# Strided sparse attention and a rational MLP: new transfer times and landing allowance in the planner, casts released by the preceding batch's loads, constant matmuls in TensorE's early rests

## The chip, the core and the metric

The kernel runs on one core of a Trainium2 chip. The metric is the device time of one execution in microseconds (us). Below, PE is the matrix engine (TensorE), DVE the vector engine, ACT the scalar engine, POOL the engine that issues casting DMAs here, and SP the engine that issues the other DMAs. The first three compute; POOL and SP hardly do anything but issue transfers. Each engine runs its own instructions strictly in the order in which the program lists them, and waits at an instruction until the semaphores that it names have their counts.

## The reference

Attention over 8 batches of 8 heads with 576 positions of 64 values, followed by an MLP on all 4608 tokens (512 wide, 2048 in the middle) whose activation is a ratio of polynomials. The first four heads (kind L) see the last 32 positions; the other four (kind S) see every 32nd position.

```python
rel = pos[:, None] - pos[None, :]
mask_local = (rel >= 0) & (rel < stride)
mask_strided = (rel >= 0) & (pos[None, :] % stride == pos[:, None] % stride)
...
attn = np.exp(scores)
attn = attn / (np.sum(attn, axis=-1, keepdims=True) + 1e-09)
return np.matmul(attn, v).astype(np.float32)
...
h = x @ w_in
P = a[0] + a[1] * h + a[2] * h2 + a[3] * h3
Q = 1.0 + np.abs(b[0]) * np.abs(h) + np.abs(b[1]) * h2
g = P / (Q + 1e-06)
return (g @ w_out).astype(np.float32)
```

The heads' outputs of a token, side by side, are its row of x.

## The kernel before

**Who sets the order.** No engine's order is written out by hand. The functions below record operations (`P.op`) with an engine, a planned duration, a key and the tiles that they read and write. `schedule` then places them: it keeps a planned time for each engine, takes the operation that is ready with the smallest key, and assigns PSUM banks on the way. A DMA has two planned times: what its issue takes on the issuing engine, and `dma=`, what the transfer takes in that engine's queue; it counts as landed (`o.fin`) 2.2 us after its transfer ends. So a planned time costs nothing itself. It decides what stands before what on each engine.

**Stages of a batch b.** `casts(b)` issues from POOL the transfers that turn q, k and v from float32 to bfloat16. For batches 0 and 1 (`b < NPE`) they go to SBUF and PE transposes them (`loads_pe`, L615 and L652, copied out at L634, L636, L664, L666). From batch 2 on, `bulk` (L517) casts in DRAM: five transfers (q, k, v for the L heads, q, k for the S heads), and two more (L572) bring v of the S heads straight to the tile vS. `loads(b)` then issues from SP two DMA transposes of q and k for each kind (L681, tiles tq, tk), four copies that swap halves of tq and tk (L692) and five loads of v (L705, L709, tile vL). `attention(b)` works on four units, L, S, S, L. Each has scores on PE (L791, L800 for L; L876, L884 for S), their negated maximum on DVE (L810, L891), its addition on PE (L817, L898), the exponential on ACT (L823, L904), a transpose of the probabilities (tiles ptL, ptS; by PE for batches 0 and 1, L835 and L916 with copies at L721 and L723; by a DMA transpose from SP after that, L841 and L924), the product with v on PE (L853; L947 with sums L934), and the division on DVE (L862, L864; L954, L957). `turn` transposes the result on PE (L747, L754), and ACT copies it into XT (L770).

**MLP.** As soon as 512 tokens (a chunk c) are in XT, `mlp1(c)` and `mlp2(c)` are recorded. `mlp1` makes two groups of eight products (L982, 4 matmuls each, copied by ACT at L988 to a tile h), and on each group of 128x4096 values DVE does nine operations (L1008, L1010, L1012, L1039, L1041 to L1045) and ACT two (L1036 Ln, L1038 Exp). `mlp2` multiplies with the second weight (L1071), ACT copies to a tile os (L1083, four in turn) and POOL stores it (L1090). The last group of the last chunk is cut up, with parts of its activation on ACT (L1004 to L1031).

**Waits that the recording adds.** `after=` makes an operation wait for others besides those of its tiles. `casts(b, after)` takes seven such lists, one for each cast and each half of vS. `loads(b, pace=land)` makes the first transposes of batch b wait for `land[0]`, the landed transposed probabilities of the first unit of the batch before, the copies and v loads for `land[1]`, and the second transposes for `land[2]`. In the main loop the casts of batch 3 wait partly for the loads of batch 2 and partly for its `land`, and those of batches 4 to 7 for `land` of the batch two before.

**Constant matmuls.** `filler` (L136 of the profile) issues matmuls on a tile FL of constants into a PSUM bank that nobody uses. `schedule` puts them where PE's plan has a rest over 0.5 us ahead of an operation with a key below −1e9 (no operation has one) or at least 8*512+2250 (the last chunk's second product): `int(rest * 0.75 / 0.216)` of them, none at time 0.

Of the kernel before, what the change touches and what calls it, by code (L numbers as in the profile page):

```python
# [84 lines left out]
class Prog:  # L85
# [65 lines left out]
    def schedule(self):  # L151
# [7 lines left out]
        free = {e: 5.0 if e == "pool" else 0.0 for e in self.ENG}  # L159
# [61 lines left out]
        while left:  # L221
# [23 lines left out]
            if e == "pe" and (o.key < -1000000000.0 or o.key >= (8 * 512 + 2250)) and t - free[e] > 0.5:  # L245
                spare = [i for i in range(8) if not held[i] and bank_free[i] <= free[e] + 0.2]
                if spare:
                    i = spare[-1]
                    n = int((t - free[e]) * 0.75 / 0.216) if free[e] > 0 else 0
                    if n:  # L250
                        bank_free[i] = max(bank_free[i], t)
                        f = self.filler(n, i, bank_tile[i], t)
                        if bank_tile[i] is None:
                            bank_tile[i] = PTile("fl", 1)
                            bank_tile[i].ops.append(f)
            free[e] = t + o.dur
            if o.dma is not None:
                at = max(dmafree[e], t + o.dur)
                busy = any(v > at for k, v in dmafree.items() if k != e)
                dmafree[e] = at + o.dma * (2 if busy else 1)  # L260
                o.fin = dmafree[e] + 2.2
            else:
                o.fin = t + o.dur
# [106 lines left out]
def bass_strided_sparse_attn__then__act_rational_pade_kernel(nc, q, k, v, moe_w_in, moe_w_out, moe_a, moe_b, out):  # L370
# [143 lines left out]
    def bulk(s_t, d_t, b, h0, nh, hd, t, key, after):  # L514
# [5 lines left out]
            0.7, key, w=[t], dma=1.65 * nh / 4, after=after)  # L520
# [14 lines left out]
    def casts(b, after=None):  # L535
# [6 lines left out]
        for n in range(2):  # L542
            if b < NPE and n:
# [5 lines left out]
                    0.8, key, w=[vt], dma=0.8, after=vl.prev)  # L549
                for h in range(HL):  # L550
# [4 lines left out]
                        1.1, key, w=[vt], dma=1.6, after=vl.prev)  # L555
# [3 lines left out]
            for i, (s_t, d_t, t) in enumerate(((q, q16, T_q[b][n]), (k, k16, T_k[b][n]))):  # L559
                if b >= NPE:  # L560
# [6 lines left out]
                    0.8, key, w=[t], dma=2.0, after=list(after[3 * n + i]) + h.prev)  # L567
# [3 lines left out]
        for x in range(2):  # L571
# [4 lines left out]
                0.9, key, w=[vS], dma=2.0, after=after[5 + x])  # L576

    def weights_in():
        FH = Fmid // 2
        for i in range(2):  # L580
            T_win[i].new()
            for kk in range(NK1):
                P.op("pool", lambda e, kk=kk, i=i: e.dma_start(
                    Win[:, kk, FH * i:FH * i + FH], w_in[kk * 128:(kk + 1) * 128, FH * i:FH * i + FH]),
                     0.8, -9e4, w=[T_win[i]], dma=1.4)

    def weights_out(after=()):
        T_wout.new()
        for j in range(4):
# [3 lines left out]
                0.8, -4e4, w=[T_wout], dma=3.3, after=after)  # L593
# [505 lines left out]
    for b in range(B):  # L1099
# [4 lines left out]
        if b == NPE:  # L1104
            g = [cur["ops"]] * 3 + [[land[0]]] * 2 + [[land[1]]] * 2
            casts(b + 1, g)
        if NPE <= b + 1 < B:
            st = loads(b + 1, pace=land if b >= NPE else None)
        if b >= NPE and b + 2 < B:
            casts(b + 2, [[land[i]] for i in ((1, 2, 2, 3, 3, 3, 3) if b == NPE else (0, 0, 1, 2, 2, 3, 3))])  # L1110
# [49 lines left out]
```

## Time and profile before

| | us |
|---|---|
| three runs, median (lowest, highest) | 427.37 (423.12, 430.69) |
| the profiled execution, its time | 427.88 |
| its span | 426.1 |
| PE busy | 376.9 (88%) |
| DVE busy | 359.2 (84%) |
| ACT busy | 291.9 (69%) |
| POOL busy | 70.7 (17%) |
| DMA transfers, median from issue to landing: transpose of q or k / of ptL / of ptS | 6.6 / 3.6 / 3.8 |
| the same, cast of q / of k / of v in DRAM | 6.2 / 7.7 / 5.7 |

The profile is of one execution. "Busy" is the time in which an engine executes; the rest is waiting or idle. The span runs from the first instruction to the end of the last; the execution's time is 1.78 us longer. PE's busy time counts matmuls as their records show them, with ends that are modelled; a mean of 393 ns stands for one of the 128x512 matmuls, which follow each other every 0.22 us at full clock. "Granted clock" is the share of its full clock that PE was given. A line such as L982 is a line of the program; a group of one line is one kind of instruction.

### The profile page before, as it was taken

What the parts mean: (1) busy time and instruction counts of PE and PEld (TensorE: products, weight loads), DVE (VectorE), ACT (ScalarE), POOL (GpSimd) and SP (SyncE); (2) the same over time, 40 slices, a digit from 0 to 9 for tenths busy, and PEclk for the clock granted to TensorE, in tenths of its full rate; (3) what the DMA queues carried; (4) which work ended last, traced back from release to release, by engine and by line L of the source; (5) the groups of instructions that cost most, each with busy time, mean ns of one, the idle gap of its engine ahead of it and who ended that gap; (6) DMA issues with size and microseconds to landing.
All of it is one profiled execution on the core that took longest, in us unless ns stands there. A gap on an engine that the chain in (4) does not pass through costs nothing.

```text
span 426.1 us, 8697 instructions
## 1 busy us (share of the span) xinstructions
PE 376.9 (88%) x3842; PEld 190.8 (45%) x3842; DVE 359.2 (84%) x315; ACT 291.9 (69%) x316; POOL 70.7 (17%) x112
## 2 busy tenths in 40 slices
PE   2777959989978598999998899989989999999796
PEld 2353536435534354554544355545444443344242
DVE  3471699999996128989999988999999999999992
ACT  2253795679465057778676848798587987989971
POOL 8951001001330012121030102000200200101100
PEclk9996996999975799899999989999999999999999
DMA  9999999106999999999699935901310110200202
GB/s 105 186 187 192 223 153 144 29 2 114 189 184 136 131 205 145 156 233 148 128 224 152 114 57 141 196 2 51 100 31 2 57 43 25 75 2 0 100 0 98
DMA packets 101830, 47.48 MB, mean 111 GB/s; under 512 B 89280, under 2 KB 97728, under 8 KB 101312
## 3 DMA queue, kind: packets, MB, share of 16 engines
q0 software_dynamic: 20384, 27.05, 36.4%
q1 hardware_dynamic: 81408, 19.87, 30.2%
q8 instruction: 30, 0.49, 0.5%
q14 instruction: 8, 0.07, 0.0%
HBM read 40.18 MB, written 18.28 MB: 137 GB/s over the span
## 4 chain that ended last, share of the span: by engine, by line
DVE 45%; PE 27%; ACT 10%; DMA 10%; issue 5%; SPq 3%; DVEq 0%; POOLq 0%
PE PSUM L982 9%; PE PSUM L1071 8%; DVE u L1012 6%; DVE h L1045 5%; DVE z L1043 5%; DVE u L1010 4%; ACT u L1036 4%; DMA ptS<-pS 4%; DVE z L1008 3%; DVE z L1041 3%; DVE xS L957 3%; DVE z L1042 3%; DVE z L1039 3%; ACT u L1038 3%; DVE z L1044 3%
## 5 line engine op out<-in xcount | busy, mean ns | idle before, releaser
L982 PE MATMUL PSUM<-XT,Win 128*128 128x512 bf16 x576 | 141.3, 393 | 4.0 <-ACT h L988 2.6
L1071 PE MATMUL PSUM<-Wout,h 128*128 128x512 bf16 x576 | 136.5, 388 | 6.3 <-DVE h L1045 4.0
L988 ACT ACTIVATE h<-PSUM 128x512 bf16<-128x512 f32 x144 | 83.0, 602 | 42.9 <-PE PSUM L982 42.9
L1071 PEld LDWEIGHTS PSUM<-Wout,h 128*128 128x128 bf16 x576 | 55.5, 99 | 73.2 <-DVE h L1045 3.8
L982 PEld LDWEIGHTS PSUM<-XT,Win 128*128 128x128 bf16 x576 | 54.0, 101 | 73.8 <-ACT h L988 11.4
L1036 ACT ACTIVATE u<-u,consts 128x4096 bf16<-128x4096 bf16 x17 | 63.1, 3710 | 15.2 <-DVE u L1012 15.2
L1038 ACT ACTIVATE u<-u 128x4096 bf16<-128x4096 bf16 x17 | 61.5, 3619 | 0.4
L1090 POOL DMA_DIRECT2D out_dram<-os x32 | 21.9, 686 | 179.6 <-ACT os L1083 179.6
L1012 DVE TENSOR_TENSOR u<-u,z 128x4096 bf16<-128x4096 bf16 x18 | 41.2, 2292 | 0.5
L1043 DVE TENSOR_TENSOR z<-z,h 128x4096 bf16<-128x4096 bf16 x17 | 39.0, 2291 | 0.5
L1041 DVE TENSOR_TENSOR z<-z,h 128x4096 bf16<-128x4096 bf16 x17 | 38.9, 2290 | 0.5
L1045 DVE TENSOR_TENSOR h<-z,u 128x4096 bf16<-128x4096 bf16 x17 | 38.9, 2286 | 0.4
L1083 ACT ACTIVATE os<-PSUM 128x512 f32<-128x512 f32 x34 | 19.2, 600 | 18.4 <-PE PSUM L1071 18.4
L1008 DVE TENSOR_SCALAR z<-h 128x4096 uint16<-128x4096 uint16 x17 | 20.6, 1213 | 12.7 <-ACT h L988 12.7
L770 ACT ACTIVATE XT<-PSUM 128x576 bf16<-128x576 bf16 (+2 forms) x40 | 19.8, 556 | 11.4 <-PE PSUM L754 8.8
L517 POOL DMA_DIRECT2D q<-in_q_dram x12 | 7.3, 610 | 110.2 <-DMA ptL<-pL 70.9
L891 DVE TENSOR_REDUCE ng<-PSUM 100x16 bf16<-100x576 f32 x16 | 11.9, 751 | 15.8 <-PE PSUM L884 15.8
L1010 DVE TENSOR_SCALAR u<-z,coef 128x4096 bf16<-128x4096 bf16 x18 | 24.1, 1338 | 0.4
L823 ACT ACTIVATE pL<-PSUM 128x960 bf16<-128x960 f32 x16 | 15.5, 966 | 12.2 <-PE PSUM L817 12.2
L1039 DVE TENSOR_SCALAR z<-h,coef 128x4096 bf16<-128x4096 bf16 x17 | 22.9, 1345 | 0.5
L904 ACT ACTIVATE pS<-PSUM 100x576 bf16<-100x576 f32 x16 | 10.2, 646 | 18.2 <-PE PSUM L898 18.1
L1044 DVE TENSOR_SCALAR z<-z,coef 128x4096 bf16<-128x4096 bf16 x17 | 21.8, 1284 | 0.5
(80 smaller groups left out, 394.0 us busy)
## 6 DMA issues: line engine op xcount, KB each, us to landing
out_dram<-os POOLq DMA_DIRECT2D x32, 256.0 KB, 3.2
q<-in_q_dram POOLq DMA_DIRECT2D x12, 288.0 KB, 6.2
k<-in_k_dram POOLq DMA_DIRECT2D x12, 288.0 KB, 7.7
vS<-in_v_dram POOLq DMA_DIRECT2D x16, 144.0 KB, 9.2
vL<-v SPq DMA_DIRECT2D x24, 96.0 KB, 6.1
Win<-in_moe_w_in_dram POOLq DMA_DIRECT2D x8, 256.0 KB, 12.7
Wout<-in_moe_w_out_dram POOLq DMA_DIRECT2D x4, 512.0 KB, 23.6
v<-in_v_dram POOLq DMA_DIRECT2D x6, 288.0 KB, 5.7
```

What stands on the lines that cost most here:

```text
L982: r = e.matmul(ph.f, Win[:, kk, f * 128:(f + 1) * 128], XT[:, kk, xc:xc + CH], start=(kk == 0), stop=(kk == NK1 - 1))
L988: P.op("act", lambda e, f=f, ph=ph, h=h: e.activation(h.t[:, f % G, :], ph.f, AF.Copy), 0.6, key, r=[ph], w=[h])
L1010: dv(lambda e, zz=zz, uu=uu: e.tensor_scalar(uu, zz, b1_ap, b0_ap, op0=Alu.mult, op1=Alu.add), ts + 0.28, r=[z, T_b], w=[u])
L1012: dv(lambda e, zz=zz, uu=uu: e.tensor_tensor(uu, uu, zz, op=Alu.mult), tt, r=[z], m=[u])
L1036: P.op("act", lambda e, uu=uu: e.activation(uu, uu, AF.Ln, bias=eps1, scale=1.0), 0.833 * W / 1000 + 0.28, key, r=[T_co], m=[u])
L1038: P.op("act", lambda e, uu=uu: e.activation(uu, uu, AF.Exp, scale=-1.0), 0.833 * W / 1000 + 0.19, key, m=[u])
L1039: dv(lambda e, zz=zz, hh=hh: e.tensor_scalar(zz, hh, a_ap[3], a_ap[2], op0=Alu.mult, op1=Alu.add), ts + 0.28, r=[h, T_co], m=[z])
L1041: dv(lambda e, zz=zz, hh=hh: e.tensor_tensor(zz, zz, hh, op=Alu.mult), tt, r=[h], m=[z])
L1043: dv(lambda e, zz=zz, hh=hh: e.tensor_tensor(zz, zz, hh, op=Alu.mult), tt, r=[h], m=[z])
L1044: dv(lambda e, zz=zz: e.tensor_scalar(zz, zz, a_ap[0], None, op0=Alu.add), ts + 0.22, m=[z])
L1045: dv(lambda e, zz=zz, hh=hh, uu=uu: e.tensor_tensor(hh, zz, uu, op=Alu.mult), tt, r=[z, u], m=[h])
L1071: r = e.matmul(po.f, h.t[:, j, m * 128:(m + 1) * 128], Wout[:, kk, :], start=(kk == 0), stop=(kk == NF - 1))
```

## The change

Four edits. The planned issue and transfer times of the POOL transfers are other numbers, POOL starts at 3.5 instead of 5.0 in the plan, and a DMA that is issued in the plan after 12 us counts as landed 1.5 us later, after 60 us 9 us later. The casts of batch 3 wait for the loads of batch 2 alone (the last vL load and the transposes of k of both kinds), those of batch b + 2 for the loads of batch b + 1; the loads no longer wait for `land`. Constant matmuls are also put into planned rests before operations with a key below 1300 (batches 0 and 1, the first products of chunk 0, and the scores at the head of batch 2), 0.7 of the rest instead of 0.75, and 16 of them ahead of PE's first operation. In the program as built there are 36 of them in the head (16, 8, 2, 2, 5, 3), and at the end 31 and 7 where there were 27 and 15.

```diff
--- before.py
+++ after.py
@@ -156,7 +156,7 @@
                 d.users.append(o)
         pend = {e: [] for e in self.ENG}
         avail = {e: [] for e in self.ENG}
-        free = {e: 5.0 if e == "pool" else 0.0 for e in self.ENG}
+        free = {e: 3.5 if e == "pool" else 0.0 for e in self.ENG}
         order = self.order = {e: [] for e in self.ENG}
         dmafree = {e: 0.0 for e in self.ENG}
         for o in list(self.ops):
@@ -242,11 +242,11 @@
             if at > t:
                 heapq.heappush(pend[e], (at, o.key, o.idx, o))
                 continue
-            if e == "pe" and (o.key < -1000000000.0 or o.key >= (8 * 512 + 2250)) and t - free[e] > 0.5:
+            if e == "pe" and (o.key < 1300 or o.key >= (8 * 512 + 2250)) and t - free[e] > 0.5:
                 spare = [i for i in range(8) if not held[i] and bank_free[i] <= free[e] + 0.2]
                 if spare:
                     i = spare[-1]
-                    n = int((t - free[e]) * 0.75 / 0.216) if free[e] > 0 else 0
+                    n = int((t - free[e]) * 0.7 / 0.216) if free[e] > 0 else 16
                     if n:
                         bank_free[i] = max(bank_free[i], t)
                         f = self.filler(n, i, bank_tile[i], t)
@@ -258,7 +258,7 @@
                 at = max(dmafree[e], t + o.dur)
                 busy = any(v > at for k, v in dmafree.items() if k != e)
                 dmafree[e] = at + o.dma * (2 if busy else 1)
-                o.fin = dmafree[e] + 2.2
+                o.fin = dmafree[e] + 2.2 + (9 if t > 60 else 1.5 if t > 12 else 0.0)
             else:
                 o.fin = t + o.dur
             order[e].append(o)
@@ -517,7 +517,7 @@
         P.op("pool", lambda e: e.dma_start(
             bass.AP(tensor=d_t, offset=(b * hd + h0) * S * D, ap=[[c, n // c], [1, c]]),
             bass.AP(tensor=s_t.tensor, offset=s_t.offset + (b * H + h0) * S * D, ap=[[c, n // c], [1, c]])),
-            0.7, key, w=[t], dma=1.65 * nh / 4, after=after)
+            0.55, key, w=[t], dma=1.4 * nh / 4, after=after)
 
     vS_of = {}
     vL_of = {}
@@ -546,13 +546,13 @@
                 VB = v.offset + b * H * S * D
                 P.op("pool", lambda e: e.dma_start(
                     vl.t[:, 0, :, 0:64], bass.AP(tensor=v.tensor, offset=VB, ap=[[D, KW], [S * D, HL], [1, D]])),
-                    0.8, key, w=[vt], dma=0.8, after=vl.prev)
+                    0.8, key, w=[vt], dma=0.6, after=vl.prev)
                 for h in range(HL):
                     P.op("pool", lambda e, h=h: e.dma_start(
                         vl.t[:, 1:NQ, h, 0:64],
                         bass.AP(tensor=v.tensor, offset=VB + (h * S + STRIDE) * D,
                                 ap=[[D, KW], [64 * D, NQ - 1], [1, D]])),
-                        1.1, key, w=[vt], dma=1.6, after=vl.prev)
+                        0.8, key, w=[vt], dma=0.95, after=vl.prev)
             if b < NPE:
                 h = stage[b, n] = R_h.next()
                 hv = h.t[:, :, :].rearrange("p g c -> p (g c)")
@@ -564,7 +564,7 @@
                     hv[0:TP, i * HL * TW:(i + 1) * HL * TW].rearrange("p (h c) -> p h c", c=TW),
                     bass.AP(tensor=s_t.tensor, offset=s_t.offset + (b * H + HL * n) * S * D,
                             ap=[[TW, TP], [S * D, HL], [1, TW]])),
-                    0.8, key, w=[t], dma=2.0, after=list(after[3 * n + i]) + h.prev)
+                    0.8, key, w=[t], dma=1.75, after=list(after[3 * n + i]) + h.prev)
             if n == 0 and b >= NPE:
                 bulk(v, vs, b, 0, HL, HL, T_v[b], key, after[2])
         vS = vS_of[b] = R_vS.next()
@@ -573,7 +573,7 @@
                 vS.t[64 * x:64 * x + SB, :, :, :].rearrange("t h g d -> t h (g d)"),
                 bass.AP(tensor=v.tensor, offset=v.offset + ((b * H + HL) * S + 8 * x) * D,
                         ap=[[16 * D, SB], [S * D, HL], [1, 8 * D]])),
-                0.9, key, w=[vS], dma=2.0, after=after[5 + x])
+                0.7, key, w=[vS], dma=0.6, after=after[5 + x])
 
     def weights_in():
         FH = Fmid // 2
@@ -582,7 +582,7 @@
             for kk in range(NK1):
                 P.op("pool", lambda e, kk=kk, i=i: e.dma_start(
                     Win[:, kk, FH * i:FH * i + FH], w_in[kk * 128:(kk + 1) * 128, FH * i:FH * i + FH]),
-                     0.8, -9e4, w=[T_win[i]], dma=1.4)
+                     0.55, -9e4, w=[T_win[i]], dma=1.2)
 
     def weights_out(after=()):
         T_wout.new()
@@ -590,7 +590,7 @@
             P.op("pool", lambda e, j=j: e.dma_start(
                 Wout[:, 4 * j:4 * j + 4, :],
                 w_out[512 * j:512 * j + 512, :].rearrange("(a p) n -> p a n", p=128)),
-                0.8, -4e4, w=[T_wout], dma=3.3, after=after)
+                0.75, -4e4, w=[T_wout], dma=2.55, after=after)
 
 
     NB = SC // TP
@@ -1102,12 +1102,12 @@
         if b == 0:
             casts(NPE)
         if b == NPE:
-            g = [cur["ops"]] * 3 + [[land[0]]] * 2 + [[land[1]]] * 2
+            g = [cur["ops"]] * 7
             casts(b + 1, g)
         if NPE <= b + 1 < B:
-            st = loads(b + 1, pace=land if b >= NPE else None)
+            st = loads(b + 1)
         if b >= NPE and b + 2 < B:
-            casts(b + 2, [[land[i]] for i in ((1, 2, 2, 3, 3, 3, 3) if b == NPE else (0, 0, 1, 2, 2, 3, 3))])
+            casts(b + 2, [st["ops"]] * 7)
         while nxt < NCH and (nxt + 1) * CH <= (b + 1) * S:
             gr, early = mlp1(nxt)
             if b + 1 < NPE:
```

## The prediction

> **What bounds the kernel now.** I read the shares of the engines first. DVE is busy 359.2 of 426.1 us, and the chain that ended last lies on it for 45%. No other engine comes near that from 170 us on. So the question is where DVE rests, and I cut the span into stretches. Columns: PE, weight loads, DVE, ACT, POOL busy, then the granted clock, DMA share, GB/s.
>
> ```profile
> core 0: us, PE busy (x) PEld busy (x) DVE busy (x) ACT busy (x) POOL busy (x), PEclk, DMA share, GB/s
> 0.00:46.00 46.00, 30.67 (x479) 18.19 (x480) 18.88 (x40) 17.55 (x30) 27.25 (x45) 0.93 1.39 170
> 46.00:120.00 74.00, 66.62 (x822) 36.28 (x819) 72.13 (x66) 52.25 (x60) 7.22 (x12) 0.95 0.75 123
> 120.00:170.00 50.00, 39.46 (x536) 20.78 (x535) 27.72 (x31) 26.57 (x34) 9.30 (x14) 0.80 1.07 156
> 170.00:403.50 233.50, 221.56 (x1935) 107.58 (x1933) 225.82 (x169) 185.15 (x189) 26.96 (x41) 0.98 0.47 92
> 403.50:426.10 22.60, 18.56 (x79) 7.92 (x79) 14.61 (x12) 10.40 (x7) 0.00 (x0) 0.94 0.15 57
> ```
>
> DVE's idle time is span less busy: 27.1 us in the head, 1.9 us from 46 to 120, 22.3 us from 120 to 170, 7.7 us up to 403.5, 8.0 us in the tail. A full stretch, 200 to 220, has 0.28 idle in 20. The chain in order of time (start, us, what) says what holds the 22.3:
>
> ```profile
> 138.60 4.51 issue
> 143.55 1.22 PE PSUM L884 x32
> ...
> 149.27 5.82 DMA ptS<-pS
> 156.93 9.01 DMA tk<-tk
> ```
>
> Three transfers in a row. The first is hidden in "issue", so I looked at the landings of what SP issued between 120 and 140:
>
> ```profile
> tq<-q SPq DMA_TRANSPOSE x1, 13.5
> tk<-k SPq DMA_TRANSPOSE x1, 18.1
> ```
>
> The transpose of the second half of k for batch 3 was issued at 124.94 and landed at 143.0. PE, in order, stood before the score L876 from 138.0 to 143.12. Then come ptS of batch 3 (149.3 to 155.1) and the swapped tk of batch 4 (156.9 to 165.9). The clock stood at 0.50 from 124 to 136 and from 144 to 150, and what ran there ran at half rate. Why was k late? The waits (total, times, longest) show POOL holding casts back for the transposed probabilities of the same batch:
>
> ```profile
> POOL q L517 <- DMA ptL<-pL: 70.9, 5, 28.1
> DVE ng L891 <- PE PSUM L884: 15.8, 3, 10.0
> DVE z L1008 <- ACT h L988: 12.7, 2, 12.3
> ```
>
> The last of these is the head: DVE starts its long work (L1008) only at 46.30. From the timeline of the head:
>
> ```profile
> 16.04 0.98 PE L791 MATMUL PSUM<-ML,IDN 128*128 128x480 bf16 x2
> 36.23 9.41 PE L982 MATMUL PSUM<-XT,Win 128*128 128x512 bf16 x32 [0.74 <-ACT XT L770]
> 52.77 0.58 PE L791 MATMUL PSUM<-ML,IDN 128*128 128x480 bf16 x2
> ```
>
> The same pair L791 takes 0.98 us at 16 and 0.58 at 52: PE runs at half rate until about 20. The 32 matmuls L982 take 9.41 us, although the last 21 of them run at some 0.22 each. The granted clock per microsecond (PE busy, clock, DMA share, GB/s) reads:
>
> ```profile
> 33.00:34.00 1.00, 0.00 (x0) 1.00 2.24 171
> 34.00:35.00 1.00, 0.96 (x13) 0.57 1.73 181
> ...
> 40.00:41.00 1.00, 1.00 (x4) 0.51 1.23 203
> 41.00:42.00 1.00, 1.00 (x6) 1.00 1.25 209
> ```
>
> **The change, part by part.** The sum starts from the profiled execution: 427.88 us, of which 426.1 is the span; the median of the three runs is 427.37, so they agree.
>
> *Planner's transfer times and the 9 us allowance.* They issue nothing. They change the order, so I read the order of the changed program as built. What counts is DVE work between the first score reduction of a batch (L891 or L810) and the first use of its transposed probabilities (the reciprocal L954 or L862). I priced the instructions between by their rows (L1012, L1041, L1043, L1045 2.29; L1010, L1039 1.35; L1042, L1044 1.29; L1008 1.22; L810 1.16; L864 0.82; L891 0.75). Before, batches 2, 3 and 4 have 12, 3.6 and 13 us. After, batches 2 to 7 have 23, 19.5, 17, 19.5, 19.5 and 19.5 us. The way from reduction to use is 0.75 + 0.45 (L898) + 0.65 (L904) + 1.3 (SP issue) + landing. ptS lands in 2.7 to 7.1, ptL in 2.9 to 14.4, so the way is 6 to 10.3 us, at worst 17.6. All but the worst is covered.
>
> *Casts released by the preceding batch's loads.* Casts 3 are released by the loads of batch 2, landed near 71. They go out together instead of three at 70.75 and the rest at 100.4, 111.5 and 123.2. Uncontended, such casts landed in 3.9 to 5.8, so all are in by about 82. The loads of batch 3 then wait on SP only behind ptL0, ptS0 and ptS1 of batch 2. By DVE's order (41.2, below, plus 37.1 us of instructions) batch 2's first reduction stands at 78, so these loads go out near 85. The loads of batch 2 took 51.58 to 70.75 = 19.2 us, so they are in near 104. The first reduction of batch 3 follows 38 us of DVE work after that of batch 2, at 116: 12 us to spare. Batch 4 comes out at 13. SP loses its waits for landed probabilities (the removed pace). On POOL, stores L1090 of a chunk's later rows now stand behind waiting casts; their tile os is next written a chunk later, over 30 us of DVE work on, and a store lands in 3.2, so I price this at 0; if casts were later than that, ACT's os copies would stop by the excess. On SP, ptL1 of batch 2 stands behind two transposes and four vL loads, about 10 us (issues 1.3 to 4.9 and 0.6 to 1.8); its use on PE has 68 long matmuls, 15 us, ahead.
>
> So of the 22.3 idle, 50 us at the full stretches' rate (0.28 in 20) keep 0.7: 21.6 come back. Unknown new waits I bound by 0 and by one like L891's longest, 10.0; nearest is the rest of the span, whose worst 20 us (240 to 260) hold 2.05, so I take 2. Net −19.6.
>
> *Sixteen first matmuls.* FL is filled by 1.43. Sixteen take 3.5 us at 0.222 (the row of L136: 27 in 5.99) or 6.8 at the half rate 0.427, so they end between 5.0 and 8.3; the transposes L615 they precede wait for h until 8.07. Cost 0 to 0.2, and then L615 for k, L791, L800 run at full rate: 0.45 + 0.4 + 0.4 = 1.2 us off the path to the first reduction. I do not count it apart: what follows waits for a landing at 18.5.
>
> *Order of the head.* The second half of tk0 (L636, four copies) now precedes the copy ptL0 on DVE. Its input landed at 18.5 (issue 7.42 + 11.1), so the copies end near 20.9 instead of 24.43 and the first L876 starts near 21 instead of 24.48. Keeping the 11.75 us from there to L982, that is 32.8; fillers of 2, 2, 5 and 3 stand on this way, 0 to 2.7 us at 0.222 if every one ends late; most stand in rests of 1.3 to 1.5, so I take 1.0: L982 at 33.8 instead of 36.23, −2.5.
>
> *Clock at L982.* If PE stays warm, 32 × 0.216 = 6.9 instead of 9.41: −2.5. L1008 starts at 41.2 instead of 46.3. Bounds for the head: −0.8 (fillers 2.7 late, clock falling) to −6. [...]
>
> *Tail.* In the new order L1010 and L1012 of the last group precede L1045 of the one before, 3.6 us. PE's L1071 on that product (8.38 us from 403.52) then ends at 415.5, and seven fillers (1.6) end at 417.1, where the last L1071 could start at 415.0: +2.1, or +0.8 if the clock does not fall before it.
>
> Sum: 427.9 − 19.6 − 2.5 − 2.5 + 2.1 = 405.4, say **405**.
>
> **Rivals.** *A late landing remains* (17%): one ptL at 14.4 or a load in contention stops PE once for some 10 us, like 10.0 now; 405 + 10 = 415. For it: landings of 13.5 and 18.1. Against: those came while casts, loads and probabilities overlapped, which the new release separates.
>
> *The clock falls anyway* (10%): at 34 to 41 the clock is 0.50 as now, 405 + 2.5 = 407.5, or 409 if the first sixteen gain nothing either. The fillers fill about half of the rests only. [...]
>
> *The change does not do what it says* (10%): allowances move the stall to other batches, DVE still loses about 20 us: 425.
>
> *The ring becomes the bound* (8%), slower. Casts now wait for loads, loads for casts: nothing of one batch overlaps the next. Ring: casts 10 + loads; DVE's work per batch is 38 to 41 us (as summed above). With loads of 19 the ring is 29 and hidden. Loads of batch 3 took 100.19 to 143.0 = 43 now. From 30 us on the ring decides; at 38, twice the undisturbed ones, each of batches 3 to 7 loses 8: 405 + 40 = 445. Against: the 43 held waits for probabilities that are gone.
>
> **Numbers.** Forecast 55% (398 to 412 by its bounds. Cheap: head −1, no new waits −2, tail −1.3, half of the 7.7 idle after 170 gone too. Dear: head +4.2, new waits of 4 instead of 2.) The range 398 to 421 takes in the late landing and the clock; it leaves out 425 and 445. Two per cent is about what a measurement can tell from no change: below 418.8, above 435.9. Faster: 55 + 10 + 13 of the 17 = 78%; same 10 + 4 = 14%; slower 8%.
>
> **What would show it.** Right: DVE busy over 9 in each 10 us from 45 to 390, no clock below 0.9 between 110 and 170, casts in blocks of seven on POOL, L1008 first near 41, L982's 32 in about 7 us. Wrong: a DVE rest over 4 us behind L934, L853 or L876, a load of a batch taking over 30 us, or L136 ending after what it precedes could start.

## The result, and the profile after

| | before | changed |
|---|---|---|
| median of the runs, us | 426.69 (423.12 to 430.69, 4 runs) | 404.61 (403.94 to 405.03, 4 runs) |
| profiled execution, us | 427.88 (span 426.1) | 404.71 (span 402.9) |
| DVE busy in the span, us | 359.2 | 359.2 |

The changed kernel takes 0.9508 of the time before, with a 95% interval of 0.9445 to 0.957; the medians lie 22.1 us apart. The four runs of the changed kernel lie within 1.1 us of each other, those of before within 7.6. Here and below a ratio and its interval compare only those runs of a kernel that lie within 1.5% of its fastest, while the medians take in all runs; where too few such runs are left, no interval is given.

DVE does the same work, so the 23.2 us by which the span is shorter are rests of DVE that are gone. The same stretches as before the change show where (columns: PE, weight loads, DVE, ACT, POOL busy, granted clock, DMA share, GB/s):

```profile
core 0: us, PE busy (x) PEld busy (x) DVE busy (x) ACT busy (x) POOL busy (x), PEclk, DMA share, GB/s
0.00:46.00 46.00, 40.18 (x602) 22.32 (x602) 24.01 (x46) 21.77 (x40) 27.26 (x45) 0.96 1.42 168
46.00:120.00 74.00, 66.19 (x946) 35.94 (x946) 73.17 (x70) 55.19 (x61) 13.18 (x18) 0.98 0.91 159
120.00:170.00 50.00, 47.54 (x472) 23.12 (x460) 47.27 (x38) 37.73 (x40) 8.52 (x11) 0.97 0.91 153
170.00:380.00 210.00, 201.59 (x1797) 97.34 (x1795) 202.98 (x154) 167.20 (x172) 25.39 (x38) 0.99 0.45 92
380.00:402.90 22.90, 18.23 (x71) 7.53 (x71) 11.74 (x11) 9.54 (x7) 0.00 (x0) 0.86 0.12 46
```

DVE's idle time is span less busy. In the head it is 22.0 us (27.1 before), from 46 to 120 it is 0.8 (1.9), from 120 to 170 it is 2.7 (22.3), up to 380 it is 7.0 (7.7, up to 403.5 there), and in the tail 11.2 (8.0). One stretch gave back 19.6 us, the head 5.1, the two stretches beside it 1.7, and the tail took 3.2.

The head by the timeline (start, us, engine, line, operation), which answers to the 9.41 us of L982 before:

```profile
33.10 7.08 PE L982 MATMUL PSUM<-XT,Win 128*128 128x512 bf16 x32 [0.28 <-ACT XT L770]
...
40.85 1.23 DVE L1008 TENSOR_SCALAR z<-h 128x4096 uint16<-128x4096 uint16 x1 [9.62 <-ACT h L988]
```

The 32 matmuls L982 run at 0.22 us each from the first, and DVE's long work starts at 40.85 instead of 46.30. The tail, by the same view:

```profile
369.94 6.85 PE L136 MATMUL PSUM<-FL 128*128 128x512 bf16 x31
378.27 2.28 DVE L1045 TENSOR_TENSOR h<-z,u 128x4096 bf16<-128x4096 bf16 x1
380.70 9.81 PE L1071 MATMUL PSUM<-Wout,h 128*128 128x512 bf16 x32 [3.90 <-DVE h L1045]
...
390.34 1.67 PE L136 MATMUL PSUM<-FL 128*128 128x512 bf16 x7
391.85 7.07 PE L1071 MATMUL PSUM<-Wout,h 128*128 128x512 bf16 x32
```

The 31 constant matmuls end at 376.8, TensorE rests 3.90 us, and the next 32 take 9.81 us, where the last 32 take 7.07. The last L1071 can start only at 391.85.

POOL's casts, with what ended the rest before them:

```profile
71.10 0.53 POOL L517 DMA_DIRECT2D q<-in_q_dram  x1 [39.66 <-DMA tk<-k]
...
110.78 0.54 POOL L1090 DMA_DIRECT2D out_dram<-os  x1 [3.46 <-ACT os L1083]
111.32 1.12 POOL L517 DMA_DIRECT2D q<-in_q_dram  x1
```

The casts of batch 3 go out in one block from 71.10 when the loads of batch 2 have landed. Those of batch 4 go out at 111.32, not when the loads of batch 3 have landed, but when the store ahead of them on POOL is let go. The same holds for batches 5 to 7, whose casts start at 149.98, 186.54 and 223.20, each straight behind a store. So they still meet transfers of the batch that is being computed, namely its ptS:

```profile
114.36 2.36 POOL L572 DMA_DIRECT2D vS<-in_v_dram  x2
...
118.98 6.35 SPq L924 DMA_TRANSPOSE ptS<-pS  x2
```

SyncE takes 6.35 us to issue this pair, where the pair at 84.75, 8 us after the last cast, took 3.02. Between 60 and 290 the landings of ptS take (least, median, longest)

```profile
DMA to landing us min/median/max: 2.7/6.0/11.1
```

against 2.7, 3.8 and 7.1 before. The longest is that of 228.82, right behind the casts of 223.20. No wait of TensorE for a ptS is on record in this stretch: they are late, but covered.

Last, the chain that ended last, shares by engine:

```profile
DVE 69%; PE 18%; ACT 5%; issue 3%; DMA 3%; POOL 2%; DVEq 0%; POOLq 0%
```

Before, DVE held 45% of the chain and transfers 10%.

### The profile page after: what moved, and what is told of

Same layout as the page of the kernel before. It is cut to its first block, busy times and chain, and to the rows that moved or that the text cites. A ratio compares the mean times of both kernels' runs of the same rounds, so it can differ in the third digit from the quotient of the medians.

```text
span 402.9 us, 8748 instructions
## 1 busy us (share of the span) xinstructions
PE 373.7 (93%) x3874; PEld 186.3 (46%) x3874; DVE 359.2 (89%) x315; ACT 291.4 (72%) x316; POOL 74.3 (18%) x112
## 4 chain that ended last, share of the span: by engine, by line
DVE 69%; PE 18%; ACT 5%; issue 3%; DMA 3%; POOL 2%; DVEq 0%; POOLq 0%
DVE u L1012 9%; DVE h L1045 8%; PE PSUM L1071 8%; DVE z L1041 8%; DVE z L1043 7%; DVE u L1010 6%; PE PSUM L982 6%; DVE z L1039 5%; DVE z L1008 4%; DVE z L1044 4%; DVE z L1042 4%; DVE xS L957 4%; DMA h<-in_k_dram 3%; DVE xL L864 2%; DVE ng L810 2%
## 5 line engine op out<-in xcount | busy, mean ns | idle before, releaser
L1071 PE MATMUL PSUM<-Wout,h 128*128 128x512 bf16 x576 | 137.8, 390 | 4.7 <-DVE h L1045 3.9
L982 PE MATMUL PSUM<-XT,Win 128*128 128x512 bf16 x576 | 136.0, 384 | 3.3 <-ACT h L988 1.3
L1071 PEld LDWEIGHTS PSUM<-Wout,h 128*128 128x128 bf16 x576 | 56.0, 100 | 72.8 <-issue 10.7
L982 PEld LDWEIGHTS PSUM<-XT,Win 128*128 128x128 bf16 x576 | 52.0, 98 | 70.5 <-ACT h L988 12.2
L1090 POOL DMA_DIRECT2D out_dram<-os x32 | 20.7, 650 | 259.8 <-ACT os L1083 259.6
L1012 DVE TENSOR_TENSOR u<-u,z 128x4096 bf16<-128x4096 bf16 x18 | 41.2, 2289 | 0.4
L1083 ACT ACTIVATE os<-PSUM 128x512 f32<-128x512 f32 x34 | 19.6, 606 | 17.5 <-PE PSUM L1071 17.4
L1008 DVE TENSOR_SCALAR z<-h 128x4096 uint16<-128x4096 uint16 x17 | 20.7, 1217 | 11.5 <-ACT h L988 11.5
L770 ACT ACTIVATE XT<-PSUM 128x576 bf16<-128x576 bf16 (+2 forms) x40 | 19.6, 560 | 7.5 <-PE PSUM L754 5.0
L136 PE MATMUL PSUM<-FL 128*128 128x512 bf16 x74 | 21.4, 446 | 1.5 <-DVE FL L503 1.5
L1044 DVE TENSOR_SCALAR z<-z,coef 128x4096 bf16<-128x4096 bf16 x17 | 21.9, 1286 | 0.6
L1042 DVE TENSOR_SCALAR z<-z,coef 128x4096 bf16<-128x4096 bf16 x17 | 21.9, 1287 | 0.4
L957 DVE TENSOR_TENSOR xS<-PSUM,rc 100x512 bf16<-100x512 f32 x32 | 20.6, 685 | 1.6 <-PE PSUM L947 1.3
L810 DVE TENSOR_REDUCE ng<-PSUM 128x10 bf16<-128x960 f32 x16 | 18.3, 1151 | 4.0 <-PE PSUM L800 3.8
## 6 DMA issues: line engine op xcount, KB each, us to landing
vS<-in_v_dram POOLq DMA_DIRECT2D x16, 144.0 KB, 10.5
```

The source lines that it names most:

```text
L982: r = e.matmul(ph.f, Win[:, kk, f * 128:(f + 1) * 128], XT[:, kk, xc:xc + CH], start=(kk == 0), stop=(kk == NK1 - 1))
L1012: dv(lambda e, zz=zz, uu=uu: e.tensor_tensor(uu, uu, zz, op=Alu.mult), tt, r=[z], m=[u])
L1042: dv(lambda e, zz=zz: e.tensor_scalar(zz, zz, a_ap[1], None, op0=Alu.add), ts + 0.22, m=[z])
L1071: r = e.matmul(po.f, h.t[:, j, m * 128:(m + 1) * 128], Wout[:, kk, :], start=(kk == 0), stop=(kk == NF - 1))
```

## Experiments

First theory: each part of the change gains by itself, the release by separating the casts from the other transfers, the allowance by distance on DVE between a batch's first reduction and the use of its probabilities. Three kernels do one part alone, and a fourth leaves one out.

**The release alone** (old planned times, no allowance, no early matmuls; only these lines differ from before):

```diff
-            g = [cur["ops"]] * 3 + [[land[0]]] * 2 + [[land[1]]] * 2
+            g = [cur["ops"]] * 7
-            st = loads(b + 1, pace=land if b >= NPE else None)
+            st = loads(b + 1)
-            casts(b + 2, [[land[i]] for i in ((1, 2, 2, 3, 3, 3, 3) if b == NPE else (0, 0, 1, 2, 2, 3, 3))])
+            casts(b + 2, [st["ops"]] * 7)
```

> The kernel before with the new release of the casts (and loads without pace) alone; old transfer times, no allowance, no early constant matmuls. Its order leaves 9 to 21 us of DVE work between a score reduction and the use of its transposed probabilities in batches 2 to 5, and 5 to 13 in batches 6 and 7. My theory (release and allowance each remove a part of the stall: the release ends the overlap of casts, loads and probabilities, the allowance gives the distance): a gain of 8 to 16 us, about 414 where before has 426.7, with rests of some 2 to 5 us left in batches 6 and 7; L1008 still near 46. Rival A (the allowance does all of it): no change, 424 to 428, the stall only moved. Rival B (the release does all of it): the whole 21 us of the middle, 405 to 407.

Measured: 426.44 us median (419.12 to 435.34, 10 runs) beside 425.99 for the kernel before; ratio 0.9941, interval 0.9871 to 1.0012. No change that can be told: the theory's gain did not come, and the time is that of rival A. Landings did not stay short either: L681 took up to 13.9 us, ptL up to 15.6.

**The planned times and the allowance alone** (old release, pace kept, no early matmuls; besides this line, the eight planned times of the change):

```diff
-                o.fin = dmafree[e] + 2.2
+                o.fin = dmafree[e] + 2.2 + (9 if t > 60 else 1.5 if t > 12 else 0.0)
```

> The kernel before with the new planned transfer times and the allowance for late landings alone; old release of the casts with its pace, no early constant matmuls. Its order leaves 16 to 23 us between reduction and use in batches 2 to 5 and 10 to 22 in 6 and 7, but puts 56 us of DVE work between the first scores of batches 3 and 4. Head as in the change but with the clock falling before L982. My theory: the middle's stall goes mostly, some 15 us, and the head gains 2 to 3: 408 to 412. Rival A (the allowance does all of the middle): 21 + 3 = 24 less, 402 to 405. Rival B (the release does all): only the head's 3, 423 to 425.

Measured: 477.07 us (476.49 to 479.97), ratio 1.1235, interval 1.1163 to 1.1307. Slower by an eighth, which neither the theory nor a rival had. The chain of waits in time order (start, us, what), then SyncE's queue in the timeline:

```profile
96.45 1.11 PE PSUM L982 x6
97.57 21.16 DMA ptL<-pL
118.73 0.04 issue
118.77 0.77 PE PSUM L853 x20
```

```profile
98.21 0.53 POOL L517 DMA_DIRECT2D q<-in_q_dram  x1
...
99.37 12.70 SPq L681 DMA_TRANSPOSE tq<-q  x1
```

A transpose of probabilities that was issued while casts went out landed after 21.16 us, and the transpose behind it took 12.70 us to issue. TensorE stood in order before L853, with the next L982 behind it.

**The early matmuls alone**:

```diff
-            if e == "pe" and (o.key < -1000000000.0 or o.key >= (8 * 512 + 2250)) and t - free[e] > 0.5:
+            if e == "pe" and (o.key < 1300 or o.key >= (8 * 512 + 2250)) and t - free[e] > 0.5:
-                    n = int((t - free[e]) * 0.75 / 0.216) if free[e] > 0 else 0
+                    n = int((t - free[e]) * 0.7 / 0.216) if free[e] > 0 else 16
```

> The kernel before with the constant matmuls in the early rests alone (16, 8, 2, 3, 5, 3 of them in the head). My theory: PE is at full clock from 8 us on and at L982, whose 32 matmuls take 7.1 instead of 9.4 us; L1008 starts near 43 instead of 46.3, the rest as before: 422 to 424. [...]

Measured: 427.35 us median, but 418.25 to 435.90 in 4 runs, so no interval is given and a gain of 5 us can't be told from none. The profiled run (418.25, the shortest of the four) shows the head's step all the same: the 32 matmuls L982 take 7.08 us, where the kernel before has 9.41, the clock is 1.00 from 20 to 42, and L1008 starts at 41.2 instead of 46.3. The rest from 120 on is still there: DVE is busy 30.6 of the 50 us to 170.

**The changed kernel without the early matmuls** (the same lines put back; with 0.75 instead of 0.7 the tail then has 33 constant matmuls instead of 31):

> The changed kernel without the constant matmuls in the early rests (at the end 33 and 7 of them as in the change's order). Its DVE order is that of the change. My theory: the matmuls before 20 us run at half rate again, and the clock is 0.50 from about 31 to 38, so the 32 of L982 take 9.4 us; L1008 at 43.5 to 45 instead of 40.9 and the time 3 to 4 us longer than the change's 404.6: 407.5 to 408.5. Rival (the gain of the head came from the order alone): 404 to 405.5, L982 at 7.1 us.

Measured: 407.84 us (407.15 to 409.94), ratio 0.9601, interval 0.9527 to 0.9675: 3.2 us over the changed kernel, as expected. Its head in stretches of 1 us and by the timeline:

```profile
32.00:33.00 1.00, 0.40 (x6) 0.41 (x7) 0.54 (x1) 0.00 (x0) 0.74 (x2) 0.50 3.24 140
...
36.00:37.00 1.00, 1.00 (x4) 0.34 (x3) 0.00 (x0) 0.22 (x1) 0.00 (x0) 0.50 1.33 176
```

```profile
35.25 8.37 PE L982 MATMUL PSUM<-XT,Win 128*128 128x512 bf16 x31 [1.14 <-ACT XT L770]
```

The granted clock is 1.00 up to 31, 0.50 from 32 on and so when L982 begins, and in 36 to 37 four matmuls fill the microsecond. (The trace has 31 of the 32.) The rests of TensorE on the way there are 0.77, 1.01 and 1.49 us. With the early matmuls the clock is 1.00 from 20 to 42.

So the parts do not add up: alone, the release is worth 0 and the plan −51, and together with the early matmuls +22. The next kernels each put one part back in the changed kernel, with two new theories, A (collision) and B (pace).

**The casts' old release** in the changed kernel (the first and last pair of the release's lines put back):

> The changed kernel, but the casts of batches 3 to 7 are released again by landed probabilities; the loads' pace stays removed. Theory A (collision: casts that go out on a landed ptL or ptS are in flight together with the next ptL and with the loads' transposes, which then land late; the allowance's order then lets TensorE stand in order before the late landing and keeps the MLP's next group waiting): landings of 15 to 21 us as with the allowance alone, time 430 to 477 us. Theory B (pace: it is the loads' wait for landed probabilities on SyncE's queue that did the harm, casts are harmless): 404 to 410 us, ptL landing in under 8 us.

Measured: 430.84 us median, 414.06 to 438.65 in 4 runs, no interval. The loads' transposes L681 landed in up to 25.8 us between 60 and 290 (6.6 in the changed kernel) and ptL in up to 15.4 (7.1). This is A's picture; two of the four runs lie in A's range and none in B's. The trace is of an execution of 434.88; the shortest run, 414.06, of which there is no trace, is still 9 us over the longest of the changed kernel.

**The loads' pace** in the changed kernel:

```diff
-            st = loads(b + 1)
+            st = loads(b + 1, pace=land if b >= NPE else None)
```

> The changed kernel, but the loads of batches 3 to 7 wait again, each for a landed transpose of probabilities of the batch before (the pace). The casts keep their new release. Theory A (collision of casts and probabilities): casts still go out only behind the loads, so landings stay under 10 us; by the order as built only batch 7 has little VectorE work between its first reduction and its use (some 5 us for a way of 6 to 10), which costs up to 5 us: 405 to 410 us. Theory B (the pace did the harm): 430 to 477 us, with transposes of SyncE held behind landed probabilities and rests of VectorE of 3 us and more in several batches.

Measured: 445.69 us (441.32 to 446.99), ratio 1.0493, interval 1.0418 to 1.0569. B's time, but not B's picture: no landing is late (L681 up to 6.9 us, ptL 4.7), and DMA holds 2% of the chain:

```profile
DVE 49%; PE 33%; ACT 10%; issue 3%; DMA 2%; POOL 1%; DVEq 0%; ACTq 0%; POOLq 0%
```

The timeline shows a DVE rest of 12.35 us with no transfer near it:

```profile
205.75 2.29 DVE L1045 TENSOR_TENSOR h<-z,u 128x4096 bf16<-128x4096 bf16 x1
...
212.55 2.13 PE L1071 MATMUL PSUM<-Wout,h 128*128 128x512 bf16 x8
...
214.52 5.34 PE L982 MATMUL PSUM<-XT,Win 128*128 128x512 bf16 x24
...
221.38 0.76 DVE L891 TENSOR_REDUCE ng<-PSUM 100x16 bf16<-100x576 f32 x1 [12.35 <-PE PSUM L884]
```

DVE finished the last h of one MLP group at 208.0; in TensorE's order the products L1071 on that h, the next group's L982 and then the next batch's scores stood one behind the other, until 221. The order had run out of work for DVE. Neither A nor B says that.

**No allowance** in the changed kernel:

```diff
-                o.fin = dmafree[e] + 2.2 + (9 if t > 60 else 1.5 if t > 12 else 0.0)
+                o.fin = dmafree[e] + 2.2
```

> The changed kernel without the allowance of 1.5 and 9 us on planned landings. By the order as built VectorE then has 6 to 16 us of work between a batch's first reduction and the first use of its probabilities, instead of 16 to 23. Theory A: landings stay short, since casts are apart; the way from reduction to use is 6 to 10 us, so a few batches fall short by 0 to 4 us each: 405 to 413 us. Rival C (the allowance does the work, the release only makes it possible): 418 to 427 us, like the release alone, which was no faster than before. Rival D (the allowance does nothing once the casts are apart): within 1 us of 404.6.

Measured: 435.11 us (433.50 to 436.77), ratio 1.0262, interval 1.0203 to 1.0321: slower than every theory said, and slower than before. Landings hold 16% of the chain. The longest such piece between 55 and 180 is

```profile
130.41 0.66 ACT pS L904
131.08 11.89 DMA ptS<-pS
143.02 0.38 PE PSUM L934 x8
```

which went out just when POOL issued five casts (130.29 to 132.7). The release does not keep casts and probabilities apart, here as in the changed kernel, and by this order as built DVE has 6 to 16 us of work to cover a landing, not 16 to 23. TensorE waits 12.2 us in all for ptS and 6.9 for ptL between 60 and 290; in the changed kernel no such wait is on record.

**The old planned times** in the changed kernel (the allowance stays; eight constants put back, such as `dma=2.0` for 0.6 on L572):

> The changed kernel with the old planned transfer times and issue costs; allowance, release and early matmuls stay. By the order as built VectorE keeps 12 to 23 us of work between reduction and use. If the distance is what counts: 404 to 407 us. If the corrected times are needed, since the order is sensitive to them: 412 us or more, with a rest of VectorE of over 4 us.

Measured: 417.36 us (416.24 to 418.68), ratio 0.9844, interval 0.9785 to 0.9903. The second expectation: landings of the loads short (L681 up to 6.1), DMA 2% of the chain, PE 30%, and DVE busy only 9.09 of the 20 us from 120 to 140, with a longest rest there of 5.36 us, before a score reduction that waited for TensorE.

Theory E came out of the pace's run: two things must hold. Landings must be short or covered, and the order must not make DVE stand. By this theory the allowance helps the first and can spoil the second, since the planner counts it for every landing along the chain from batch to batch, and the pace lengthens that chain. (The planned rests named in the expectations are the planner's own due times; what they say of the chip is what the runs test.)

**The pace with 5 us**:

```diff
-            st = loads(b + 1)
+            st = loads(b + 1, pace=land if b >= NPE else None)
-                o.fin = dmafree[e] + 2.2 + (9 if t > 60 else 1.5 if t > 12 else 0.0)
+                o.fin = dmafree[e] + 2.2 + (5 if t > 60 else 1.5 if t > 12 else 0.0)
```

> The changed kernel with the loads' pace put back, as in the run that took 445.7 us, but with an allowance of 5 us instead of 9 on landings planned after 60 us. Theory E (the allowance is counted once for every landing along the chain from batch to batch: loads, scores, landed probabilities, and with the pace the next loads on top; 9 us on each is more than one batch's 38 us of VectorE work can take, so that the order itself makes VectorE stand until TensorE's turn comes, with no late landing at all): with 5 us the chain fits, the planned order has no rest of VectorE over 3 us between 60 and 380, and the time falls by some 35 us to 404 to 412 us. Theory F (the pace does the harm on the chip, by holding SyncE's queue, or by transfers that meet): 430 to 446 us, as with 9 us.

Measured: 399.55 us (398.95 to 400.22), ratio 0.9465, interval 0.9411 to 0.952: 46 us under the same kernel with 9 us, and under E's range. F (the pace does harm on the chip) falls. It is also the fastest kernel of the study: its highest run is 3.7 us under the lowest of the changed kernel, though the two were not measured side by side, and their intervals against the kernel before overlap.

```profile
46.00:120.00 74.00, 66.51 (x933) 36.17 (x942) 70.91 (x70) 52.05 (x60) 12.97 (x18) 0.93 1.03 167
120.00:170.00 50.00, 48.50 (x569) 25.26 (x577) 48.50 (x43) 41.38 (x42) 6.57 (x11) 1.00 0.81 157
170.00:380.00 210.00, 198.77 (x1679) 95.75 (x1705) 205.70 (x151) 168.81 (x172) 23.54 (x38) 1.00 0.40 88
```

DVE rests 4.3 us from 170 to 380 where the changed kernel rests 7.0.

**An allowance of 13 us** in the changed kernel, pace still out:

```diff
-                o.fin = dmafree[e] + 2.2 + (9 if t > 60 else 1.5 if t > 12 else 0.0)
+                o.fin = dmafree[e] + 2.2 + (13 if t > 60 else 1.5 if t > 12 else 0.0)
```

> The changed kernel with an allowance of 13 us instead of 9. Theory E: without the pace the chain from batch to batch has room for 9 us but not for 13; the order as planned then has some 28 us more of VectorE's rests than with 9, in pieces of 4 to 7 us, and the time goes to 425 to 437 us, with few landings in the chain of waits. Rival G (the allowance only puts more distance between reduction and use, and distance does no harm beyond need): 403 to 406 us.

Measured: 434.53 us (433.72 to 436.20), ratio 1.0299, interval 1.0234 to 1.0363, as E expected; G falls. The stretch and the chain's shares:

```profile
170.00:290.00 120.00, 106.45 (x1164) 54.28 (x1176) 94.29 (x79) 81.53 (x93) 18.65 (x28) 0.93 0.79 142
```

```profile
DVE 45%; PE 35%; ACT 11%; issue 4%; DMA 2%; POOL 1%; DVEq 0%; POOLq 0%
```

DVE stands 25.7 us of 120 (5.7 in the changed kernel), no landing of L681 is over 6.4 us, TensorE waits for none of the transposes, and it is TensorE's and ACT's turns that the chain runs through.

**The old release at 5 us**: as the 399.55 us version, with the casts released by landed probabilities again, to see whether the release itself does anything on the chip.

> The version with the pace and an allowance of 5 us (399.6 us), but with the casts released again by landed probabilities, as before the change. The orders as built hold alike: 14 to 20 us of VectorE's work between reduction and use in every batch here, 14 to 19 there, no planned rest of VectorE over 2 us between 60 and 380 in either. So only what the casts do on the chip differs. Theory A (casts that go out on landed probabilities are in flight beside the next ptL and the loads' transposes and make them land late): landings of ptL or of the loads' transposes of 12 us and more, shares of 8% and more for DMA and SyncE in the chain of waits, 412 to 430 us. Rival H (with 14 us of distance and no planned rest the casts' release no longer matters): 398 to 404 us.

Measured: 421.49 us median (405.40 to 428.67, 10 runs, no interval), none of the ten as fast as any of the other's four; the shortest is 5.2 us over the longest of those. In the timeline of an execution of 424.72:

```profile
114.60 0.50 POOL L517 DMA_DIRECT2D q<-in_q_dram  x1 [20.22 <-DMA ptL<-pL]
115.08 0.50 POOL L517 DMA_DIRECT2D k<-in_k_dram  x1
115.28 3.70 SPq L681 DMA_TRANSPOSE tk<-k  x1
115.58 1.29 POOL L572 DMA_DIRECT2D vS<-in_v_dram  x2
...
127.16 0.66 PE L876 MATMUL PSUM<-MS,IDN 128*128 128x288 bf16 x2 [9.86 <-DMA tk<-k]
```

A landed ptL lets casts go at 114.60; k's transpose, issued at 115.28 beside them, landed 11.84 us later, and TensorE stood 9.86 us. (Three stores of 256 KB went out at 116.86 too; what each does to the transpose is not told apart.) That is A's mechanism, and H falls: even the shortest run lies above its 398 to 404. What makes the ten runs differ by 23 us is not shown; only one was traced.

**The tail**, in the changed kernel:

```diff
-                    n = int((t - free[e]) * 0.7 / 0.216) if free[e] > 0 else 16
+                    n = int((t - free[e]) * (0.95 if o.key > 1300 else 0.7) / 0.216) if free[e] > 0 else 16
```

> The changed kernel with the constant matmuls in the rests of the last part filled to 0.95 of the planned rest instead of 0.7 (43 before the first and 9 before the second of the last two products, instead of 31 and 7). Theory (the clock of the last products falls because TensorE idles 3.9 us after the 31st, and 32 L1071 then take 9.81 us instead of about 7): the first product ends earlier, PE's end comes nearer to VectorE's, 402.0 to 403.6 us, 1 to 2.5 us under the changed kernel. Rival (the rest is shorter on the chip than planned, so more of them end after the product could start): 405 to 407 us.

Measured: 402.91 us (402.06 to 404.90, 6 runs), ratio 0.9553, interval 0.9499 to 0.9607: 1.7 us under the changed kernel, inside what was expected, but with an interval that holds the changed kernel's 0.9508, so the gain itself is not shown. The mechanism is:

```profile
370.41 9.44 PE L136 MATMUL PSUM<-FL 128*128 128x512 bf16 x42
381.16 7.07 PE L1071 MATMUL PSUM<-Wout,h 128*128 128x512 bf16 x31 [1.31 <-DVE h L1045]
```

TensorE now rests 1.31 us before L1071, which takes 7.07 instead of 9.81; the granted clock is 1.00 from 380 to 388, where the changed kernel has 0.50 from 380 to 386. (The trace has 42 of the 43 constant matmuls and 31 of the 32 products.) The 399.55 us version needs none of this: there 21 constant matmuls end 1.23 us before its last L1071, which run in 7.08.

The runs side by side: longest landing of each kind of transpose between 60 and 290 us of the profiled run, TensorE's waits there that the profile puts down to one of these landings, share of the chain on transfers and SyncE's issues, and on PE and ACT.

| kernel | us | L681, us | ptL, us | ptS, us | TensorE waited, us | DMA and SP, % | PE and ACT, % |
|---|---|---|---|---|---|---|---|
| before | 426.69 | 18.1 | 14.4 | 7.1 | 4.5 | 13 | 37 |
| planned times and allowance alone | 477.07 | 22.3 | 21.2 | 4.6 | 8.4 | 9 | 40 |
| casts' old release | 430.84 | 25.8 | 15.4 | 12.0 | 23.2 | 16 | 28 |
| old release at 5 us, pace | 421.49 | 25.8 | 9.6 | 9.8 | 22.4 | 27 | 33 |
| release alone | 426.44 | 13.9 | 15.6 | 5.9 | 10.5 | 8 | 33 |
| no allowance | 435.11 | 10.4 | 10.9 | 11.9 | 19.1 | 20 | 38 |
| old planned times | 417.36 | 6.1 | 5.6 | 10.2 | 0 | 2 | 40 |
| allowance 13 | 434.53 | 6.4 | 7.4 | 10.5 | 0 | 2 | 46 |
| pace kept, 9 us | 445.69 | 6.9 | 4.7 | 5.8 | 0 | 2 | 43 |
| changed | 404.61 | 6.6 | 7.1 | 11.1 | 0 | 3 | 23 |
| pace kept, 5 us | 399.55 | 6.3 | 10.3 | 8.6 | 0.7 | 11 | 13 |

(Of the last row's 11%, 7 points are one stretch of the head that ends at 53, before the batches in question. To the 4.5 us of the first row come 5.2 before L876, which the profile calls "issue".) The rows fall into three groups: TensorE waits for late transposes (the first six), no such wait but an order that makes DVE wait for TensorE (the next three), and the two fast kernels, which have next to nothing of either. A long landing by itself does not make a kernel slow: ptS took up to 11.1 us in the changed kernel, ptL up to 10.3 in the fastest.

## Why the prediction came out

405.0 us was forecast and 404.6 measured, and the sizes of the steps were near; that the two agree to 0.4 us is partly luck. By DVE's rests, the stretches from 46 to the tail gave 21.3 us where 19.6 was forecast, the head 5.1 (5.0), and the tail took 3.2 (2.1). The reason given for the largest step was half of the truth.

- *Middle, −19.6.* The forecast was 21.6 from 120 to 170 less 2 for new waits. The rests from 120 to 170 fell by 19.6, with 1.0 from 46 to 120 and 0.7 after 170 on top; so the same figure came out for another sum. The due points held: casts of batch 3 from 71.1 (near 71 forecast), loads of batch 3 issued from 87.8 to 101.3 (from 85, in by 104), the first reduction of batch 3 at 114.6 (116).
- *What counts is DVE work between reduction and use.* The work was there: by the trace of the changed kernel batches 2 to 7 have 16 to 22 us (17 to 23 forecast). (Before, batch 3 had 8.8 us by the trace, where the prediction counted 3.6.) But this test was not enough. With some 12 to 24 us of such work by the trace in batches 2 to 7 the allowance of 13 took 434.5, and with 15 to 18 the pace at 5 us took 399.6. The prediction did not look whether the order lets DVE stand elsewhere, in MLP groups that wait for TensorE's turn. The changed kernel's order does not, and the run with 13 shows how near the edge it is. The rival that allowances move the stall to other batches (425 us) was given 10%; something like it, DVE standing for TensorE's turn instead of for a landing, is what three of the neighbours do.
- *The release separates the transfers.* In part. Pairs with the old and new release differ, 421.5 against 399.6 and 430.8 against 404.6 (shortest runs 405.4 against 399.0 and 414.1 against 403.9), and what the new release keeps apart from the casts, in the kernels with an allowance, are the loads' transposes: L681 lands in 6.9 us at most instead of up to 25.8. The casts still meet ptS, in the changed kernel too (up to 11.1 us). There the distance that the allowance made covers it; without an allowance TensorE stood for it.
- *SP's removed pace* was told as a gain. What is shown is that its removal lets the plan bear 9 us (404.6 against 445.7); with 5 us it is part of the fastest kernel.
- *POOL's stores priced at 0.* Right in price. The held side was the other one: the casts of batches 4 to 7 waited behind a store. Their landings were early enough all the same, but the wait (for batch 4 from about 104, when the loads of batch 3 had landed, to 111.3) brought them nearer to ptS; what that costs was not tried apart. The rival that the ring of casts and loads becomes the bound has nothing for it: the loads of batch 3 took some 16 us from the first issue to the last landing (87.8 to about 104), against 43 before.
- *Head, −5.0.* L876 at 20.59 (21), L982 at 33.10 (33.8) in 7.08 (6.9), L1008 at 40.85 (41.2), so −5.45. The sixteen first matmuls ended at 8.0, inside 5.0 to 8.3, and L615 then waited for its input until 9.0, not for them. The run without early matmuls gives them 3.2 us of the total. There the clock fell to 0.50 on the way to L982, where TensorE rested 0.77, 1.01 and 1.49 us between 27.47 and 32.60, as before the change, with rests of 1.29 and 1.49 us between 30.55 and 34.04. In the tails it fell in longer ones: some 2.7 us into the rest of 3.90 us in the changed kernel, and before the change some 2.2 us into one of 2.95.
- *Tail, +2.1.* Mis-sized: TensorE ended 8.2 us after DVE's last product, 5.2 before the change, so +3.0. The forecast took 8.38 us for the L1071 on the product before, as in the old tail; it took 9.81, since the 31 constant matmuls ended 3.90 us early and the clock stood at 0.50 for longer (from about 379.5 until after 386, against 402.8 until after 406).
- *The signs named.* L1008, L982 and the casts in blocks came as said. Two signs of being right failed in places: DVE is busy 8.7, 8.7, 7.9 and 8.9 of the 10 us from 120, 170, 210 and 270, and the clock is 0.83 from 150 to 160. One sign of being wrong came, as the forecast's own tail has it: the seven constant matmuls hold the last L1071 to 391.85, 1.1 us after DVE's last product.
- *Two slips.* The cheap bounds add up to 397.3, not 398. And PE comes near DVE by its records from 170 to 403.5 (221.6 against 225.8 us busy); it is the chain, not the busy time, that makes DVE the bound there.

What stays open: which dependence of the plan carries the allowance into a rest was read from the code and not tried one by one. Few values of the allowance were tried (5 us without the pace was not), so a time that rises and falls smoothly with it is not shown, and that some other order of the same list would do as well is not excluded. The scatter of the kernels with the old release (up to 25 us between runs) was not traced.

## What to carry to other kernels

A constant in a list scheduler that stands for late transfers can cost more than the late transfers (9 and 5 us with the pace: 445.7 and 399.6). A reading that fits the runs with 5, 9 and 13 us, but was not shown step by step, is that it is paid once per landing on the chain from one stage to the next. Try several values, and for each look at two things: whether an engine waits for a landing, and whether the bounding engine waits for another engine's turn with no transfer near. Edits to one order do not add up; each of the five parts put back alone cost between 3 and 41 us, of a gain of 22, so judge them by leaving one out as well as by doing one alone. Release bulk copies on an event after which the transposes that an engine will wait for are done, not on one that announces the next of them (with an allowance, L681 landed in 6.9 us at most the one way, in up to 25.8 the other), look in the trace whether that event is what lets them go (here it was a store ahead of them), and plan enough work to cover those that they still meet.

## What the runs showed of the hardware

Each engine began its instructions in the order of the program: in the trace of the changed kernel all 3874 matmuls of TensorE, all 315 instructions of DVE and all 316 of ACT stand in that order. Transposes by DMA land in some 3 to 5 us (ptL, median 3.0 to 4.6 in ten of the eleven kernels above, 6.7 in the other), but took 11.1 (changed kernel, ptS), 11.8 (old release at 5 us, tk), 11.9 (no allowance, ptS) and 21.2 us (planned times and allowance alone, ptL) where casts of 288 KB went out just before or beside them, and SyncE then, in the last of these, took up to 12.70 us to issue one instead of 1.3. The granted clock fell to 0.50 in the head of the kernel before (1.00 at 33 to 34, 0.57 at 34 to 35, with rests of 1.29 and 1.49 us from 30.55 to 34.04) and of the changed kernel without the early matmuls (1.00 at 30 to 31, 0.50 at 32 to 33, with rests of 0.77, 1.01 and 1.49 us from 27.47 to 32.60); with 2, 5 and 3 constant matmuls from 27.9 to 32.8, in the changed kernel, it is 1.00 from 20 to 42. It also fell within single rests of 2.95 us (kernel before) and 3.90 us (changed), some 2.2 and 2.7 us into them. It did not in single rests of 1.23 and 2.78 us (399.55 us version, 32 products in 7.08 us after each) and 1.31 (0.95 in the tail, 7.07). Rests alone do not settle it: in the changed kernel it stood at 0.50 from about 11 to 14 us, with one rest of 1.0 us shortly before. And in the first 8 us the view gives a clock of 1.00, although sixteen matmuls of 128x512 take 6.53 us there, 0.41 each instead of 0.22.
